# Releasing the loads of granules 8 and 9 by the last attention average instead of the landed transposes, in a fused attention and MoE kernel

## The chip, the cores and the metric

The kernel runs on one core of one Trainium2 chip. The metric is the device time of one execution in microseconds (us); lower is better. The kernel before takes 210.3 us (median of 3 runs, 210.06 to 210.32). A profiled execution has a span about 1.8 us shorter than its time, because the span begins with the first instruction of the program.

## The reference

Attention with a few global keys and a local window, then a two-layer MLP whose activation is `s * relu(x)^2 + b`. The attention is shortened here to its steps; the MLP is as in the reference:

```python
def _attn_ref(q, k, v, n_global, n_local):      # q, k, v: 4 x 8 x 768 x 64
    scores = (q @ k^T) / sqrt(64) + bias         # bias: -slope(head) * distance
    keep = first 8 keys, or the 96 keys up to the query's own
    a = softmax(where(keep, scores, -1e9))
    return a @ v

def _moe_ref(x, w_in, w_out, s, b):              # x: 3072 x 512, d_ff 2048
    h = x @ w_in
    r = np.maximum(h, 0.0)
    g = s * (r * r) + b
    return (g @ w_out).astype(np.float32)
```

## The kernel before

The 3072 tokens are cut into 12 granules of 256 (j = 0 to 11). Each granule passes through: loads of k, q and v from HBM (software DMA queue, issued by GpSimd, with a cast to bf16); transposes of k and q; scores, exponent and mask; weighted averages `xn[j]` (`stage_A`, normalised by VectorE, two heads at a time); transposes of `xn[j]` to `xT[j]`; the two MLP products. From granule 4 on the transposes are DMA transposes. They are issued by the sync engine (SP) on the hardware DMA queue, which also carries the stores of the output and the copies of v blocks (`vo`).

Six loads make a granule. They are issued four granules ahead, and from granule 6 on a *gate* holds them: a one-element copy on GpSimd that reads a tile, so that the loads behind it in GpSimd's order wait until that tile is written.

```python
    def load_granule(j):
        b, g = divmod(j, NGR)
        t = nat_tile(j)
        for i in range(GB):                        # GB = 2
            sb = g * GB + i
            for n in range(2):
                nc.gpsimd.dma_start(t[:, n, i, :, :], rows_of(srcs[n], b, sb))
            nc.gpsimd.dma_start(vbuf[b % 2][:, sb, :, 0:D], rows_of(v, b, sb))

    def hold_loads(ap):
        g = work.tile([P, 1], BF16, name="gate", tag="gate")
        nc.gpsimd.tensor_copy(g[0:1, :], ap)
...
    def x_by_dma(j):
        t = xT_tile(j)
        for i in range(GB):
            nc.sync.dma_start_transpose(t[:, :, i * P : (i + 1) * P], xn[j][:, i, :])
...
    def finish_granule(j):
        if j < X_PE:                               # X_PE = 4
            x_by_pe(j)
        else:
            x_by_dma(j)
        if 6 <= j + LEAD < NJ:                     # LEAD = 4, NJ = 12
            hold_loads(xT[j][0:1, 0, GT - 1 : GT])
            load_granule(j + LEAD)

    def step(s, c0, c1, c2, pool=None, pre=()):
        j = 2 * s // HP                            # two steps a granule
        last = (2 * s + 2) % HP == 0
        if not last and j >= 4 and j + 2 < NJ:
            qk_by_dma(j + 2)                       # 4 DMA transposes on SP
        ...
        if last:
            finish_granule(j)
            if SHIFT < j + 2 < NJ:
                load_voff(j + 2)
        ...
```

So the first MLP product of a granule waits for its pair `xT(j)`, and the gate of granule j+4 waits for the same pair.

The softmax here doesn't subtract the row's maximum and nothing guards it: scores larger than these inputs give would overflow.

## Time and profile before

| | before |
|---|---|
| time, median | 210.3 us |
| span of the profiled execution | 208.7 us |
| TensorE (PE) busy | 201.1 us, 96% |
| VectorE, ScalarE, GpSimd busy | 77%, 62%, 33% |
| PE idle for a pair xT | 1.13 us, once |

First the page of the kernel before: busy time, and the span in 40 slices of 5.2 us. A digit is the busy share in tenths. In all views PE is TensorE, PEld its weight loads, DVE VectorE, ACT ScalarE, POOL GpSimd and SPq the queue of SP; L616 is line 616 of the kernel, and x16 means 16 instructions in a row.

```profile
PE 201.1 (96%) x2183; PEld 160.0 (77%) x2191; DVE 160.0 (77%) x336; ACT 128.6 (62%) x200; POOL 68.9 (33%) x89
...
PE   6899999999999999999997999999999999999993
...
DMA  5999999999999999999999999999451210240006
...
DMA packets 110308, 28.17 MB, mean 135 GB/s; under 512 B 97836, under 2 KB 108780, under 8 KB 110284
```

TensorE bounds the kernel. The only dent of the PE row in the middle is the 7 of slice 22, at about 110 to 115 us. The DMA engines are busy over 90% of the time until about 145 us, although they move only 135 GB/s on average. The Trainium skill ("DMA: Bandwidth & Descriptors", Specifications) gives 512 B as the least transfer for line rate; 97,836 of the 110,308 packets here are smaller, which fits busy engines at a low rate.

The timeline of PE in that dent (start, duration, operation; in brackets the idle time before it and what ended it), then the chain that ended last in the same place (start, duration):

```profile
109.41 3.78 PE L816 MATMUL ps<-wsub,gsum 128*128 128x256 bf16 x32
...
114.57 1.91 PE L616 MATMUL ps<-xT,w_in_bf 128*128 128x256 bf16 x16 [1.13 <-DMA xT<-xn]
```

```profile
102.54 1.93 SPq L596
104.47 0.06 issue
104.53 9.90 DMA xT<-xn
114.44 0.14 issue
114.57 1.91 PE ps L616 x16
```

The second transpose of xT(6) was issued at 104.53 and took 9.90 us to land. PE was ready at 113.4 and started at 114.57. Next GpSimd (gates and first loads behind them) and SP:

```profile
81.63 0.18 POOL L122 COPY gate<-xT 1x1 bf16<-1x1 bf16 x1 [12.18 <-DMA xT<-xn]
82.20 0.87 POOL L116 DMA_DIRECT2D nat<-in_k_dram  x1 [0.40 <-issue]
...
96.01 0.26 POOL L122 COPY gate<-xT 1x1 bf16<-1x1 bf16 x1 [8.55 <-DMA xT<-xn]
96.61 0.88 POOL L116 DMA_DIRECT2D nat<-in_k_dram  x1 [0.34 <-issue]
...
114.56 0.18 POOL L122 COPY gate<-xT 1x1 bf16<-1x1 bf16 x1 [12.69 <-DMA xT<-xn]
```

```profile
76.30 2.51 SPq L596 DMA_TRANSPOSE xT<-xn  x2
...
90.05 2.54 SPq L596 DMA_TRANSPOSE xT<-xn  x2
```

The gate of granule 8 runs 5.3 us after the first transpose of xT(4) is issued, that of granule 9 6.0 us after that of xT(5). Last, the two DMA queues from 98 to 111 us (packets, MB, time of the packets as a share of this stretch on 16 engines; packets overlap, so over 100% is possible). q0 carries the loads, q1 transposes and stores:

```profile
q0 software_dynamic: 6213, 0.78, 111.4%
q1 hardware_dynamic: 2918, 1.14, 65.7%
```

In this stretch the loads of granule 9 took more of the engines than everything on the hardware queue.

### The profile page before, as it was taken

To read this page: it belongs to the slowest core of one execution; us is meant where nothing else is said; L and a number is where in the kernel's file an instruction comes from. 1 tells how busy PE (TensorE), PEld (TensorE's weight loads), DVE (VectorE), ACT (ScalarE), POOL (GpSimd) and SP (SyncE) were. 2 spreads that over 40 slices of the span, in tenths; PEclk is the share of its full clock that TensorE was granted. 3 is DMA by queue.
4 is the path that set the end of the run, shared out by engine and by line. 5 is a ranking of instruction groups with operands and counts; after the bars stand their busy time and mean duration, and the time that the engine had idled before them with its cause. 6 is when DMAs were issued, how large, how long until landed. Compare 5 with 4: busy or idle time off the path is not lost.

```text
span 208.7 us, 5315 instructions
## 1 busy us (share of the span) xinstructions
PE 201.1 (96%) x2183; PEld 160.0 (77%) x2191; DVE 160.0 (77%) x336; ACT 128.6 (62%) x200; POOL 68.9 (33%) x89
## 2 busy tenths in 40 slices
PE   6899999999999999999997999999999999999993
PEld 2677884557867585878886898888898889888883
DVE  7685689995989866799799784599785696737974
ACT  4975669485975558685763766564966665476200
POOL 8984334999646102705500906300000000000000
PEclk9999999999999999999999999999999999999999
DMA  5999999999999999999999999999451210240006
GB/s 167 170 181 206 207 207 172 155 152 135 115 147 143 155 157 193 120 265 188 145 207 128 113 133 174 184 208 100 52 158 49 77 28 0 50 154 0 0 4 200
DMA packets 110308, 28.17 MB, mean 135 GB/s; under 512 B 97836, under 2 KB 108780, under 8 KB 110284
## 3 DMA queue, kind: packets, MB, share of 16 engines
q0 software_dynamic: 75472, 13.11, 86.7%
q1 hardware_dynamic: 33612, 14.13, 39.0%
q10 hardware_dynamic: 1200, 0.59, 1.1%
q8 instruction: 17, 0.28, 0.6%
q14 instruction: 7, 0.06, 0.1%
HBM read 27.26 MB, written 6.29 MB: 161 GB/s over the span
## 4 chain that ended last, share of the span: by engine, by line
PE 76%; DMA 9%; POOL 4%; SPq 4%; DVE 3%; issue 1%; POOLq 0%
PE ps L616 35%; PE ps L816 19%; PE ps L664 13%; DMA xT<-xn 5%; DMA w_in_bf<-in_moe_w_in_dram 5%; PE ps_s L438 4%; PE ps_av L492 4%; SPq L357 3%; POOL nat L102 2%; POOL vb L108 2%; SPq L596 1%; PE ps_t L348 1%; POOL w_in_bf L140 1%; DVE o_early L697 1%; DVE wsub L751 1%
## 5 line engine op out<-in xcount | busy, mean ns | idle before, releaser
L616 PE MATMUL ps<-xT,w_in_bf 128*128 128x256 bf16 x768 | 90.5, 273 | 1.7 <-DMA xT<-xn 1.1
L626 ACT ACTIVATE gT<-ps 128x512 bf16<-128x512 f32 x96 | 55.7, 598 | 48.4 <-PE ps L616 48.2
L616 PEld LDWEIGHTS <-w_in_bf 128*128 128x128 bf16 x768 | 72.8, 98 | 11.3 <-issue 1.2
L447 ACT ACTIVATE pt<-ps_s 128x1024 bf16<-128x1024 f32 (+1 forms) x44 | 39.3, 946 | 3.2 <-PE ps_s L438 3.2
L664 PE MATMUL ps<-w_out_bf,gT 128*128 128x512 bf16 x120 | 28.9, 379 | 0.5 <-issue 0.2
L816 PEld LDWEIGHTS <-gsum 128*128 128x128 bf16 x256 | 24.1, 98 | 3.7 <-DVE gsum L779 0.5
L454 DVE TENSOR_TENSOR pt<-pt,tmpl 128x1024 bf16<-128x1024 bf16 (+1 forms) x40 | 24.5, 644 | 1.7 <-ACT pt L447 1.6
L790 DVE TENSOR_TENSOR gT<-gT 128x1024 bf16<-128x1024 bf16 x20 | 13.7, 685 | 11.6 <-ACT gT L626 11.6
L664 PEld LDWEIGHTS <-gT 128*128 128x128 bf16 x128 | 11.7, 98 | 13.2 <-issue 0.3
L463 DVE TENSOR_TENSOR xn<-ps_av,rc 128x256 bf16<-128x256 f32 x48 | 20.4, 424 | 1.7
L116 POOL DMA_DIRECT2D nat<-in_k_dram x20 | 17.7, 886 | 8.6 <-DMA w_in_bf<-in_moe_w_in_dram 2.1
L816 PEld LDWEIGHTS <-gT 128*128 128x128 bf16 x200 | 18.7, 98 | 2.3
L117 POOL DMA_DIRECT2D vb<-in_v_dram x20 | 18.4, 919 | 5.9 <-DMA nat<-in_k_dram 2.4
L116 POOL DMA_DIRECT2D nat<-in_q_dram x20 | 17.9, 896 | 6.9 <-DMA w_out_bf<-in_moe_w_out_dram 2.9
L462 DVE RECIPROCAL rc<-ps_av 128x4 f32<-128x4 f32 x48 | 8.6, 178 | 12.8 <-PE ps_av L492 10.6
L492 PEld LDWEIGHTS <-pt 128*128 128x128 bf16 x320 | 14.4, 98 | 2.7 <-DVE xn L463 0.7
L629 DVE TENSOR_TENSOR gT<-gT 128x512 bf16<-128x512 bf16 x32 | 13.0, 420 | 3.7 <-ACT gT L626 3.3
L492 PE MATMUL ps_av<-vb,pt 128*128 128x65 bf16 x208 | 15.4, 193 | 0.0
L816 PE MATMUL ps<-w_out_bf,gsum 128*128 128x256 bf16 x128 | 15.3, 273 | 0.0
L816 PE MATMUL ps<-wsub,gsum 128*128 128x256 bf16 x128 | 15.1, 273 | 0.0
L122 POOL COPY gate<-xT 1x1 bf16<-1x1 bf16 x6 | 1.1, 190 | 40.6 <-DMA xT<-xn 39.5
L816 PE MATMUL ps<-w_out_bf,gT 128*128 128x256 bf16 x120 | 13.9, 273 | 0.0
(112 smaller groups left out, 221.8 us busy)
## 6 DMA issues: line engine op xcount, KB each, us to landing
out_dram<-o_q SPq DMA_DIRECT2D x15, 256.0 KB, 2.3
vb<-in_v_dram POOLq DMA_DIRECT2D x24, 128.0 KB, 7.4
nat<-in_k_dram POOLq DMA_DIRECT2D x22, 128.0 KB, 6.9
nat<-in_q_dram POOLq DMA_DIRECT2D x22, 128.0 KB, 7.3
w_out_bf<-in_moe_w_out_dram POOLq DMA_DIRECT2D x4, 512.0 KB, 17.2
w_in_bf<-in_moe_w_in_dram POOLq DMA_DIRECT2D x3, 512.0 KB, 11.2
out_dram<-o_sb SPq DMA_DIRECT2D x4, 256.0 KB, 6.1
out_dram<-o_early SPq DMA_DIRECT2D x4, 256.0 KB, 5.2
```

What stands on the lines that cost most here:

```text
L116: nc.gpsimd.dma_start(t[:, n, i, :, :], rows_of(srcs[n], b, sb))
L117: nc.gpsimd.dma_start(vbuf[b % 2][:, sb, :, 0:D], rows_of(v, b, sb))
L447: nc.scalar.activation(pt[:, :, 0:ncol], ps[:, :, 0:ncol], ACT.Exp, scale=QSCALE)
L454: nc.vector.tensor_tensor(pv, pv, m.rearrange("p h a c -> p h (a c)"), ALU.mult)
L463: nc.vector.tensor_tensor(dst, av[:, :, :, 0:D], rc[:].to_broadcast((P, 2, 2, D)), ALU.mult)
L492: nc.tensor.matmul(av[:, i, hi, 0 : D + 1], lhsT=pt[:, hi, c * P : (c + 1) * P], rhs=vv, start=(n == 0), stop=(n == len(terms) - 1),)
L616: nc.tensor.matmul(ps[:, i, :], lhsT=w_in_bf[:, kc, fc * P : (fc + 1) * P], rhs=xT[j][:, kc, :], start=(kc == 0), stop=(kc == KC - 1),)
L626: nc.scalar.activation(gs, ps[:], ACT.Relu)
L629: nc.vector.tensor_tensor(gs, gs, gs, ALU.mult)
L664: nc.tensor.matmul(po[:], lhsT=g_of(j)[:, fc, tb * P : (tb + 1) * P], rhs=w_out_bf[:, fc, :], start=(fc == 0), stop=(fc == FC - 1),)
L790: outs.append(lambda: nc.vector.tensor_tensor(gs, gs, gs, ALU.mult))
L816: nc.tensor.matmul(ps[:, tb, cs], lhsT=stat[:, fc, tb * P : (tb + 1) * P], rhs=mov[:, fc, cs], start=(fc == 0), stop=(fc == NH - 1),)
```

## The change

The gates of granules 8 and 9 read the last normalised average of granules 4 and 5 instead of the landed transposes of it. The intent: these loads start some 5 us earlier, and are out of the way sooner. The instruction order of every engine stays the same.

```diff
         if 6 <= j + LEAD < NJ:
-            hold_loads(xT[j][0:1, 0, GT - 1 : GT])
+            if j in (4, 5):
+                hold_loads(xn[j][0:1, GB - 1, DM - 1 : DM])
+            else:
+                hold_loads(xT[j][0:1, 0, GT - 1 : GT])
             load_granule(j + LEAD)
```

## The prediction

> **What bounds the kernel.** The page gives TensorE (PE) 201.1 us busy of a 208.7 us span (96%), at full granted clock; VectorE 160.0 (77%), ScalarE 128.6 (62%). The chain of waits is nearly all PE. Only 7.6 us of PE idleness exists, mostly at head and tail. In the stage of the change (76 to 120 us), the timeline of PE shows one long gap: 1.13 us ahead of 114.57 us, where the first MoE product of granule 6 waits for the DMA transposes of xT(6). The list of waits has the same item (1.1 us, once), and the chain shows those transposes issued to 104.5 and landed at 114.44: 9.9 us. The same pair takes 2.4 to 2.5 us late in the kernel, when no loads run. So the reachable gain is about 1.1 us, 0.5%.
>
> **What moves.** The instruction order on every engine is unchanged; only what two 1-element gate copies on GpSimd wait for changes. No arithmetic is added or removed.
> - Gate of granule 8: now at 81.63 us (landed xT(4)); it should run at about 76.3, when the last average of granule 4 is done. Its six loads (0.87 to 0.93 us issue each, now 82.2 to 87.4) move to about 76.9 to 82.2: 5.3 us earlier.
> - Gate of granule 9: now 96.01; should run near 90.1. Loads move from 96.6-101.9 to about 90.7-96: 5.9 us earlier.
> - Later gates still wait for landed transposes, but these land earlier if xT(6) does.
>
> **Gain.** Loads of granule 9 occupy the software DMA queue from 98 to about 110 us now, on top of xT(6) (issued 102.5 to 106). Moved by 6 us, they should be nearly done by 104; xT(6) then lands at about 108 to 110, before PE wants it (113.4). The 1.13 us wait goes. Gate 10 runs then, near 109 instead of 114.6, and xT(7) (6.9 us to landing now, slack over 4 us) gets easier too; no gain there, PE does not wait for it.
>
> **Cost.** The two pairs of transposes that used to be protected now share the DMA engines with the loads. The Trainium skill ("DMA: Bandwidth & Descriptors", "Queues, rings and completion order") says each DMA engine round-robins between its queues packet by packet; the trace agrees in effect: pairs beside running loads land in 4.5 to 9.9 us, pairs without in 2.4.
> - xT(4): second transpose issued at 77.55, landed at 81.6 (4.0 us; the tail of granule 7's loads ends near 79.2). PE wants it at 84.04. With loads continuing, I estimate 6 to 7 us (like xT(7) 6.9 and xT(8) 6.2): 83.5 to 84.6, so a new wait of 0 to 1 us, 0.4 expected.
> - xT(5): issued to 92.6, landed 95.9, wanted at 98.5. Loads ran beside it before too (granule 8's tail to 93.7). Estimate 97 to 98: no or a small wait.
> - The score transposes of granules 7 and 8 land later, with slack of many us. Buffers of the loads (query/key slots of granules 4 and 5, value blocks) are read out well before 76 and 90 us, so no new wait.
>
> **Sum.** -1.1 + 0.4 + 0.1 = -0.6 us: 210.3 to 209.7 us. Range 208.9 to 210.9. Faster by over 2%: 1%; within 2%: 97%; slower: 2%.
>
> **What would show it.** Gate copies at about 76.3 and 90.1; first software-queue packets of granule 8 near 78; the wait of PE for xT at 114 gone; xT(6) landing within 7 us; a PE gap of under 1 us near 84 with xT(4) as releaser.
>
> **What would make it wrong.** xT(4) or xT(5) landing in about 10 us as xT(6) does now: 2 to 4 us lost. Or another wait right behind xT(6)'s, such as a PSUM buffer, taking the gain. Or later pairs (xT(7), xT(8)) falling onto granule 10's and 11's loads at a worse moment.

## More of the kernel before

From 103 to 115 us:

```profile
q1 hardware_dynamic: 3682, 1.54, 95.7%
q0 software_dynamic: 3437, 0.43, 65.9%
```

From 104.53 to 114.43 us, while the second transpose of xT(6) was under way, the shares were 101.7% (q1) and 49.5% (q0), and from 110 to 115 us only 38 load packets ran. So the wait for xT(6) is not only a matter of loads beside it: the last score transposes and the stores ahead of it landed only at 105.2 to 111.0 us, and a copy of v blocks (`vo`), issued right behind it at 106.12 us, landed with it at 114.4.

## The result, and the profile after

The changed kernel took 209.9 us (median of 4 runs, 209.44 to 210.0) beside 210.31 us (210.06 to 210.74): ratio 0.9974, 95% interval 0.9952 to 0.9996. A ratio here is the mean time of one kernel's fast runs over that of the other's of the same rounds, so it is not quite the ratio of the medians.

The span fell from 208.7 to 208.1 us. The same lines as before, first the page:

```profile
PE 202.3 (97%) x2183; PEld 160.5 (77%) x2191; DVE 160.5 (77%) x336; ACT 128.8 (62%) x200; POOL 69.5 (33%) x89
...
PE   7999999999999999999999999999999999999993
```

The dent is gone. The timeline of PE at xT(5) and xT(6), without a bracket now:

```profile
99.11 1.92 PE L616 MATMUL ps<-xT,w_in_bf 128*128 128x256 bf16 x16
...
114.00 1.91 PE L616 MATMUL ps<-xT,w_in_bf 128*128 128x256 bf16 x16
```

The gates, the loads, and the pairs on SP:

```profile
76.80 0.31 POOL L122 COPY gate<-xn 1x1 bf16<-1x1 bf16 x1 [6.67 <-DVE xn L463]
77.40 0.88 POOL L116 DMA_DIRECT2D nat<-in_k_dram  x1 [0.29 <-issue]
...
89.47 0.57 POOL L122 COPY gate<-xn 1x1 bf16<-1x1 bf16 x1 [6.81 <-DVE xn L463]
90.09 0.88 POOL L116 DMA_DIRECT2D nat<-in_k_dram  x1
...
112.01 0.52 POOL L122 COPY gate<-xT 1x1 bf16<-1x1 bf16 x1 [16.66 <-DMA xT<-xn]
```

```profile
100.27 3.21 SPq L357 DMA_TRANSPOSE qx<-nat  x1
...
104.75 2.55 SPq L596 DMA_TRANSPOSE xT<-xn  x2
```

The two gates run 4.8 and 6.5 us earlier. And the queues from 98 to 111 us:

```profile
q1 hardware_dynamic: 4066, 1.87, 100.6%
q0 software_dynamic: 3452, 0.43, 55.0%
```

In this stretch the loads moved 0.43 MB instead of 0.78, and the hardware queue 1.87 MB instead of 1.14.

The trace has the time at which the semaphore of each DMA reached its full count. Worked out from it, for the second transpose of each pair: from issue to landing, and the slack, from landing to the start of the first product that reads the pair.

| pair | before: landing after, slack | after: landing after, slack |
|---|---|---|
| xT(4) | 4.0 us, 2.47 us | 6.0 us, 0.54 us |
| xT(5) | 4.5 us, 2.60 us | 7.0 us, 0.05 us |
| xT(6) | 9.9 us, 0.13 us (PE waited) | 5.8 us, 2.11 us |
| xT(7) | 6.9 us, 4.39 us | 7.1 us, 4.94 us |
| xT(8) | 6.7 us, 3.47 us | 4.1 us, 6.14 us |

For xT(8) before, the prediction has 6.2 us; the full count gives 6.7. A slack of 0.05 to 0.13 us is the time from landing to start when PE is released by the landing itself. So the changed kernel has moved the thin place from xT(6) to xT(5): it starts those products just as they arrive.

How to compare two spans: the two traces differ by 0.46 us before the change can act. The last group of sixteen first-layer products of granule 3, a point ahead of the first moved gate, starts at 75.43 us before and at 75.89 after. I use it as a mark. **From the mark to the end** it takes 133.28 us before and 132.24 after: 1.04 us less. The span shows only 0.6 of it, because the profiled execution of the changed kernel happened to reach the mark later. Over the 14 traces, with the same instructions up to the mark on every engine that computes (eight PE records are missing in some traces), the mark lies between 75.25 and 76.09 us.

### The profile page after: what moved, and what is told of

Same layout as the page of the kernel before. It is cut to its first block, busy times and chain, and to the rows that moved or that the text cites. A ratio compares the mean times of both kernels' runs of the same rounds, so it can differ in the third digit from the quotient of the medians.

```text
span 208.1 us, 5315 instructions
## 1 busy us (share of the span) xinstructions
PE 202.3 (97%) x2183; PEld 160.5 (77%) x2191; DVE 160.5 (77%) x336; ACT 128.8 (62%) x200; POOL 69.5 (33%) x89
## 4 chain that ended last, share of the span: by engine, by line
PE 86%; DMA 5%; POOL 4%; DVE 3%; issue 1%; POOLq 0%
PE ps L616 40%; PE ps L816 24%; PE ps L664 12%; DMA w_in_bf<-in_moe_w_in_dram 5%; PE ps_s L438 4%; PE ps_av L492 4%; POOL nat L102 2%; POOL vb L108 2%; POOL w_in_bf L140 1%; PE ps_t L348 1%; DVE wsum L642 1%; DVE pt L454 1%; PE ps_last L816 0%; PE ps_x L588 0%; DVE vo L394 0%
## 5 line engine op out<-in xcount | busy, mean ns | idle before, releaser
L616 PE MATMUL ps<-xT,w_in_bf 128*128 128x256 bf16 x768 | 90.4, 273 | 0.3 <-DMA w_in_bf<-in_moe_w_in_dram 0.3
L616 PEld LDWEIGHTS <-w_in_bf 128*128 128x128 bf16 x768 | 72.7, 98 | 10.0 <-DMA w_in_bf<-in_moe_w_in_dram 0.5
L116 POOL DMA_DIRECT2D nat<-in_k_dram x20 | 17.7, 886 | 8.3 <-DMA w_in_bf<-in_moe_w_in_dram 2.0
L117 POOL DMA_DIRECT2D vb<-in_v_dram x20 | 17.9, 894 | 5.5 <-DMA nat<-in_k_dram 2.0
L492 PEld LDWEIGHTS <-pt 128*128 128x128 bf16 x320 | 14.5, 97 | 3.0 <-DVE xn L463 0.7
L792 ACT ACTIVATE gT<-gT 128x1024 bf16<-128x1024 bf16 x12 | 12.7, 1057 | 0.4
```

The lines of the kernel that those rows point to most:

```text
L492: nc.tensor.matmul(av[:, i, hi, 0 : D + 1], lhsT=pt[:, hi, c * P : (c + 1) * P], rhs=vv, start=(n == 0), stop=(n == len(terms) - 1),)
L616: nc.tensor.matmul(ps[:, i, :], lhsT=w_in_bf[:, kc, fc * P : (fc + 1) * P], rhs=xT[j][:, kc, :], start=(kc == 0), stop=(kc == KC - 1),)
```

## The experiments

Theory T1: the gain is the end of PE's wait for xT(6), which came from granule 9's loads on the DMA engines while the hardware queue in front of xT(6) drained; the price is slack at xT(4) and xT(5). Rival R1: it helps that all loads come earlier. Rival R2: the difference is start-up scatter. After the first eight runs T1 was sharpened to T2: in the timed runs the changed kernel gives part of its gain back, since the thin slacks run out in some executions.

Every result below was correct. "To the end" is from the mark to the end; the ratio is to the kernel before on the same chip.

| run | to the end, us | PE gap at a pair xT | slack of xT(4), (5), (6), us | median us, range | ratio, 95% interval |
|---|---|---|---|---|---|
| before_again | 133.15 | xT(6) 0.99 | 3.40, 1.68, 0.13 | 210.01, 209.22 to 210.88 | 1.0001, 0.9972 to 1.0031 |
| after_again | 132.22 | none | 0.81, 0.05, 3.01 | 209.80, 209.40 to 211.24 | 1.0006, 0.9975 to 1.0037 |
| only9 | 132.54 | xT(5) 0.46 | 2.68, 0.05, 1.93 | 210.12, 209.76 to 210.31 | 1.0007, 0.9985 to 1.0028 |
| only8 | 132.07 | none | 0.74, 3.04, 0.13 | 210.01, 209.25 to 211.13 | 1.0009, 0.9978 to 1.0040 |
| extra_loads | 133.46 | xT(4) 0.74, xT(6) 0.36 | 0.13, 0.05, 0.13 | 211.00, 210.22 to 211.74 | 1.0030, 1.0001 to 1.0058 |
| late9 | 132.05 | none | 2.44, 2.67, 2.80 | 209.51, 209.23 to 209.73 | 0.9956, 0.9936 to 0.9975 |
| both_at_4 | 132.14 | none | 1.31, 0.05, 2.67 | 210.16, 209.88 to 210.35 and one of 214.38 | 0.9984, 0.9963 to 1.0006 |
| split9 | 132.32 | xT(4) 0.12, xT(5) 0.09 | 0.13, 0.05, 1.99 | 210.17, 209.35 to 210.47 | 0.9979, 0.9955 to 1.0003 |
| after_third | 132.22 | none | 0.81, 0.05, 3.42 | 210.25, 209.36 to 211.89 | 1.0000, 0.9962 to 1.0037 |
| late9_again | 132.64 | xT(8) 0.44 | 2.60, 2.49, 0.54 | 209.74, 209.23 to 210.24 | 0.9967, 0.9936 to 0.9998 |
| early8_late9 | 132.09 | none | 0.72, 3.61, 1.96 | 209.89, 209.14 to 211.32 | 0.9980, 0.9945 to 1.0015 |
| late9_extra | 132.05 | none | 2.99, 0.48, 1.31 | 209.96, 209.40 to 211.28 | 0.9984, 0.9950 to 1.0017 |

Each row has one trace and six timed runs; the trace is of the first of the six. Rows 1 to 4, 5 to 8 and 9 to 12 ran together on one chip each. The 214.38 us run is over 1.5% above the kernel's fastest, so slow, and is left out of the ratio.

### before_again and after_again: both kernels once more

No edit.

> Control: the kernel before, unchanged. All theories: ratio 1.000 within 0.2%. Its trace is a second look at the kernel before: theory T1 (the whole gain is the end of PE's wait for xT(6)) expects a PE gap ahead of the first product of granule 6 of 0.5 to 1.5 us again, xT(6) landing 8 us or more after its issue, and 133.3 +- 0.4 us from the last products of granule 3 (75.4 us) to the end. The rival R2 (the difference is start-up scatter) expects that this stretch varies by as much as the 1.04 us that separate the first two traces.

> The changed kernel again, for the size of the gain. T1: ratio 0.994 to 0.998, no PE gap for xT(6), 132.2 +- 0.3 us from the last products of granule 3 to the end, slack of xT(5) under 0.5 us. R2: ratio 0.999 to 1.001.

The traces repeat: the kernel before has the gap again, the changed kernel has not.

```profile
114.66 1.91 PE L616 MATMUL ps<-xT,w_in_bf 128*128 128x256 bf16 x16 [0.99 <-DMA xT<-xn]
```

To the end: 133.28 and 133.15 us before, 132.24, 132.22 and (after_third) 132.22 after. The two kernels are apart by seven times the difference between the repeats, so R2 fails for the profiled executions. The timed runs do not follow: the ratio was 1.0006 here and 1.0000 in after_third, after 0.9974 at first. T1's 0.994 to 0.998 is missed. The single times of the changed kernel reach 211.24 and 211.89 us, those of the kernel before, in the three chip sessions, 210.88, 211.33 and 211.57.

### only9 and only8: one half of the change at a time

```diff
-            if j in (4, 5):
+            if j in (5,):          # only9;  (4,) for only8
```

> Only granule 9's loads are released by the average (granule 5); granule 8's still by the landed xT(4). T1: this half alone carries the gain, since the loads beside xT(6) are those of granule 9: ratio as after_again within 0.15%, no PE gap at xT(6), xT(4) landing about 4 us and with its slack of about 2.5 us back. Rival R1 (both loads must come earlier, as a queue that is cleared from granule 8 on): half of the gain or less.

> Only granule 8's loads are released by the average (granule 4); granule 9's still by the landed xT(5). T1: nearly no gain, ratio 0.998 to 1.000, PE gap at xT(6) of 0.5 us or more stays, because granule 9's loads still start near 95 to 96 us. R1: half of the gain (gap about 0.5 us).

only9 removes the gap at xT(6) and gives xT(4) its slack back, as T1 said, but xT(5) then arrives 7.7 us after its issue and PE waits there:

```profile
99.45 1.92 PE L616 MATMUL ps<-xT,w_in_bf 128*128 128x256 bf16 x16 [0.46 <-DMA xT<-xn]
```

The loads of granule 8, landing until 94.8 us, and those of granule 9, issued from 89.9, now both lie beside xT(5). So "this half carries the whole gain" was too simple: about 0.7 of the 1.0 us remains (133.28 and 133.15 before, 132.54 here). only8 contradicts T1 outright: I expected a gap of 0.5 us or more, and there was none; xT(6) landed 9.0 us after its issue, but just in time. Its loads of granule 9 were all landed by 107.9 us, against 114.3 and 112.3 in the two traces of before, though issued at nearly the same time (96.2 against 96.6 and 97.8). Clearing granule 8 early also helps the next set through; R1 has a point there. One trace of each cannot say how often, and the trace of only8 is of the fastest of its six runs (209.25 us, median 210.01), as are those of both_at_4 and split9. The timed runs separate neither from the kernel before.

### extra_loads: two more loads beside xT in the changed kernel

```diff
+    spare = [const.tile([P, H, D], BF16, name=f"spare{i}", tag=f"spare{i}") for i in range(2)]
...
             load_granule(j + LEAD)
+            if j == 4:
+                for n in range(2):     # to spare tiles, not used
+                    nc.gpsimd.dma_start(spare[n][:], rows_of(srcs[n], 3, n))
```

> The changed kernel with two needless loads of 128 KB (to a spare tile) behind the six of granule 8, so that the software queue stays busy about 2.5 us longer, to about 91 to 94 us, just ahead of xT(5). T1 (the changed kernel has no slack left at xT(5): 0.05 us in two profiles): xT(5) lands 1 to 3 us late, PE shows a gap of 0.5 to 2.5 us near 99 to 101 us, 133.2 to 134.5 us from the last products of granule 3 to the end; ratio to before 1.000 to 1.007. Rival (the loads run in free time and PE does not feel them): no gap, 132.2 us, ratio as the changed kernel.

The cost came, 133.46 to the end, 1.24 us over the changed kernel, and the timed ratio is 1.003. The place was partly wrong: the gaps are at xT(4) and xT(6), not at xT(5), which again arrived just in time, after PE had been held up already. (This kernel has one line more, so L617 is L616 elsewhere.)

```profile
84.81 1.91 PE L617 MATMUL ps<-xT,w_in_bf 128*128 128x256 bf16 x16 [0.74 <-DMA xT<-xn]
...
114.83 1.91 PE L617 MATMUL ps<-xT,w_in_bf 128*128 128x256 bf16 x16 [0.36 <-DMA xT<-xn]
```

The two loads landed at 95.3 and 98.3 us, later than the 91 to 94 us expected. So PE does feel the loads, and the changed kernel has no room for more of them.

### late9: the loads of granule 9 later than before

```diff
+        if j == 6:
+            hold_loads(xn[6][0:1, GB - 1, DM - 1 : DM])
+            load_granule(9)
-        if 6 <= j + LEAD < NJ:
+        if 6 <= j + LEAD < NJ and j != 5:
             hold_loads(xT[j][0:1, 0, GT - 1 : GT])
             load_granule(j + LEAD)
```

> The opposite direction: granule 8's loads as before, granule 9's loads released later than before, by the last average of granule 6 (about 102 us in place of 96). T1 in its simple form (what hurts xT(6) is loads that run while the hardware queue in front of it, score transposes of granule 8 and two stores, drains): that queue drains alone, score transposes of granule 8 land by about 103, xT(6) beside the loads takes 6 to 7 us from about 104.3, lands at 110.5 to 111.5, no PE gap, 132.2 to 132.5 us to the end. Rival R1 (only an earlier release helps; later loads meet xT(6) more): xT(6) lands at 114 or later, gap of 1 us or more, 133.2 us or more to the end.

> The late release of granule 9 again. T2: every pair xT has 2 us or more to spare, so its runs are tight (spread under 0.8 us) and faster: ratio to before 0.994 to 0.997, median 0.2 to 0.8 us under that of after_third. If the first late9 result was the chance of one chip: ratio 0.998 to 1.001, no better than after_third.

This was the run that told most. The gate of granule 9 moves 5.7 us the other way, from 96.01 to 101.67, so that its loads begin together with xT(6) and run beside it to its landing, and the gap is gone all the same:

```profile
101.67 0.51 POOL L122 COPY gate<-xn 1x1 bf16<-1x1 bf16 x1 [13.91 <-DVE xn L463]
```

The score transposes of granule 8, ahead of xT(6) in the hardware queue, had landed by 102.5 us (107.2 before), and the two stores behind them by 104.5 (111.0 before); xT(6) then took 6.9 us, although the loads took 115.5% of the engines in that time, against 49.5% while it was under way before. The timeline of PE at xT(6), without a gap, and the queues from 98 to 111 us in late9, where the loads take 64.0% in place of 111.4%, much as in the changed kernel (55.0%):

```profile
113.56 1.91 PE L616 MATMUL ps<-xT,w_in_bf 128*128 128x256 bf16 x16
```

```profile
q0 software_dynamic: 3735, 0.47, 64.0%
q1 hardware_dynamic: 3210, 1.25, 59.5%
```

R1, which wanted 133.2 us or more, fails as the sole reason: loads need not come early. That they must not meet a backlog on the other queue fits this trace, but it is not the whole account. The other three traces with late loads also had the queue ahead clear by 105.4 us, and there xT(6) took 7.7, 8.1 and 8.9 us (early8_late9, late9_extra, late9_again), the last not far from the 9.3 and 9.9 us of before. And the changed kernel gets there by another way than T1 says: its score transposes and stores landed at 108.0 and 110.7 us, no sooner than before, but while its xT(6) was under way the loads took only 4.2% of the engines.

In late9 the three pairs keep 2.4 us or more, its six runs lie within 0.5 us, and it is the fastest kernel: 0.9956, and 0.9967 on another chip, both intervals below 1. It is no free lunch: in late9_again xT(6) had only 0.54 us left, the runs were spread over 1.01 us where T2 expected less than 0.8, and later traffic was pushed onto xT(8), which took 10.6 us.

```profile
144.72 1.91 PE L616 MATMUL ps<-xT,w_in_bf 128*128 128x256 bf16 x16 [0.44 <-DMA xT<-xn]
```

### both_at_4 and split9: earlier still, and in two parts

both_at_4 puts the loads of granule 9 right behind those of granule 8; split9 releases three loads of granule 9 by the average of granule 5 and three by the landed xT(5).

```diff
# both_at_4
-        if 6 <= j + LEAD < NJ:
-            hold_loads(xT[j][0:1, 0, GT - 1 : GT])
+        if 6 <= j + LEAD < NJ and j != 5:
+            if j == 4:
+                hold_loads(xn[4][0:1, GB - 1, DM - 1 : DM])
+            else:
+                hold_loads(xT[j][0:1, 0, GT - 1 : GT])
             load_granule(j + LEAD)
+            if j == 4:
+                load_granule(9)
# split9, in place of load_granule(9)
+                load_qk(9, 0)
+                load_v(9, [0])
+                hold_loads(xT[5][0:1, 0, GT - 1 : GT])
+                load_qk(9, 1)
+                load_v(9, [1])
```

> The loads of granules 8 and 9 both released by the average of granule 4 (about 76.7), twelve loads in a row to about 87 us, landing until about 98. T1: xT(4) as in the changed kernel (slack 0.4 to 1.0), xT(5) beside loads until about 97, lands at 98 to 100, PE gap 0 to 1 us there; xT(6) free of loads, 3 to 5 us to landing, slack 4 us or more; 132.2 to 133.2 us to the end, so between the two kernels. R1 (earlier is better throughout): 132.2 or less, no gap.

> Granule 8 by the average of granule 4 as in the changed kernel; of granule 9 the first three loads by the average of granule 5, the other three by the landed xT(5). A try at the best of both halves: T1: xT(5) lands at 96 to 98 (slack 1 to 2.5), xT(6) at 111 to 112.5 (slack 1 to 2), no PE gap, 132.2 us to the end, and fewer slow executions than the changed kernel if its 210.7 to 211.2 us runs come from xT(5); ratio 0.996 to 0.999.

In both_at_4 the loads lasted until 106.8 us, not 98, and still xT(6) had 2.7 us of slack, xT(5) none: 132.14 to the end, no better than the changed kernel. split9 did not do what I wanted: xT(5) got no slack, with granule 8's loads landing until 94.3 us and three of granule 9's beside it, and xT(4) had a gap of 0.12 us. Neither is a better kernel than late9.

### after_third, early8_late9 and late9_extra: where the changed kernel loses in the timed runs

early8_late9 is late9 with granule 8 released as in the changed kernel. late9_extra is late9 with the two needless loads of extra_loads. The edits are those above, combined.

> The changed kernel a third time, beside late9_again on the same chip. T2 (in the timed runs the changed kernel gives part of its gain back because xT(4) and xT(5) arrive with 0.0 to 0.8 us to spare, so an execution in which they are a little later stalls): ratio to before 0.996 to 1.000, spread of its runs 0.7 us or more, profile: 132.0 to 132.6 us from the last products of granule 3 to the end.

> The changed release of granule 8 (average of granule 4) with the late release of granule 9. This separates the two thin slacks of the changed kernel: xT(4) is beside loads as in the changed kernel (slack 0.1 to 0.8), xT(5) is free (slack 3 or more), xT(6) as in late9. T2: profile 132.0 to 132.4 us to the end; runs a little slower or more scattered than late9_again (ratio 0.995 to 0.999) if xT(4) causes the slow executions, equal to late9_again if they come from xT(5) alone.

> The late release with the same two needless loads behind those of granule 8 that cost the changed kernel 1.2 us in its profile. T2 (a load costs time only where it eats more than the slack of the transposes beside it): xT(4) untouched (slack 2 or more), xT(5) loses 1 to 3 of its 2.7 us, xT(6) as in late9; PE gap 0 to 0.3 us, 132.0 to 132.5 us to the end, ratio to late9_again within 0.15%. Rival (every added load costs PE time through the shared DMA engines): 133 us or more to the end, 0.4% or more over late9_again, as it did in the changed kernel.

late9_extra is the clean comparison, though with one trace: the loads that cost the changed kernel 1.24 us to the end cost late9 nothing (132.05, as late9). They took xT(5) down to 0.48 us of slack and stopped there. That is what T2 says, and the rival (every load costs) fails in this trace; in the timed runs the ratios of late9_extra and late9_again, 0.9984 and 0.9967, differ by 0.17%, just over the 0.15% expected and well inside their intervals. early8_late9 shows where each slack went: with granule 8 early alone, xT(4) is down to 0.72 us as in the changed kernel, but xT(5) has 3.61. On the slow executions T2 stays unproved: early8_late9 and late9_extra each had one run of six over 211.2 us, the changed kernel 2 of 16 (4 of 16 over 210.6), late9 none of 12. But the kernel before, counted in the same way over all sessions, had 2 of 43 over 211.2 us and 9 of 43 over 210.6, so long runs are not special to the changed kernel. These counts are too small to name xT(4) or xT(5), and none of the runs over 211.2 us was profiled.

## Why the prediction was right or wrong

The prediction said 209.7 us, 208.9 to 210.9, and within 2%; 209.9 was measured. Point by point:

- **What bounds it, and the reachable gain: right.** PE at 96%, one gap of 1.13 us at xT(6). In the traces the change takes 1.04 us from the stretch after the mark.
- **The gates: right.** Predicted at about 76.3 and 90.1, found at 76.80 and 89.47. The first loads were issued at 77.40 and 90.09.
- **xT(4): size right, consequence too dark.** Predicted to land in 6 to 7 us and to cost 0.4 us; it took 6.0 us and arrived 0.54 us before it was wanted, with no gap in three traces of the changed kernel.
- **xT(5): mis-sized.** Predicted to land at 97 to 98; it landed at 99.06 (98.6 if the late start is taken off), with all of its slack gone. The failed step is the term "loads ran beside it before too", from which I took the loads of granule 9 for no worse than the tail of granule 8's. They are worse, since they run on through the whole of its flight. In the seven traces in which granule 9's loads start beside xT(5) or earlier (the changed kernel three times, only9, split9, extra_loads, both_at_4) its second transpose takes 6.9 to 7.7 us; in the six where they start after its landing (before twice, only8, late9 twice, early8_late9) 3.4 to 5.5. early8_late9 shows that in the changed kernel it is these loads and not the earlier granule 8: with granule 8 as in the changed kernel and granule 9 late, xT(5) takes 3.4 us. Whose loads they are does not matter: in the fourteenth trace, late9_extra, granule 9 starts late too, but the two needless loads land until 98.2 us, and xT(5) takes 6.6 us. The waiting itself is small: against the mark, its products start 0.17 us later than in the kernel before (99.11 - 75.89 against 98.48 - 75.43), and 0.02 and 0.08 us in the two repeats, so the "0.1" of the sum was about right.
- **xT(6): mechanism right, size off.** The loads no longer lay on top of it (4.2% of the engines while it was under way, 49.5% before), and the wait went; late9 shows that this is not the only way to end it. It was to land at 108 to 110; it landed at 111.9. The loads of granule 9 lasted until 107.7 us, not 104: first issue to last landing took 17.6 us, as it had before (17.7 us). And SP issued the second transpose at 106.04, 1.5 us later than before, since one score transpose of granule 8 held it for 3.21 us (1.29 before; 3.42 and 3.08 in the repeats of the changed kernel, 1.23 in that of the kernel before). The gate of granule 10 ran at 112.0 instead of 109.
- **Sum: near the predicted -0.6 us in the first comparison, in part by luck.** There the means differ by about 0.55 us (0.26%) and the medians by 0.4. In the profiled executions the change is worth -1.04 us, not -0.6, because the expected 0.4 us at xT(4) did not come; the profiled execution reached the mark 0.46 us late, which has nothing to do with the change. In timed runs the three comparisons gave 0.9974, 1.0006 and 1.0000, whose mean of 0.9993 is about -0.1 us, less than predicted. So the 0.26% of the first comparison is not established, and that it came near the prediction is luck as far as these runs show. Where 1 us of gain goes in the unprofiled executions is open. That thin slack eats it fits the traces (0.05 us at xT(5) in all three) and the late9 kernel, but it is an argument, not shown. A rival is that the traces make the kernel before look worse than it is: both its profiled executions (210.51 and 210.57 us) are above the medians of their sessions (210.3 and 210.0), those of the changed kernel (209.9, 209.8 and 210.0) at or below theirs (209.9, 209.8 and 210.25). Against it, late9 removes the same gap and gains about 0.7 and 0.9 us in timed runs (0.9967 and 0.9956), so the wait seems to be there in them too.

The Trainium skill ("DMA: Bandwidth & Descriptors", Queues, rings and completion order) has each DMA engine serve its queues in turn, packet by packet. The traces agree in effect: in the kernel before, the second transpose of a pair takes 2.5 us with no loads about (xT(10), xT(11); 3.7 for xT(9), with copies of v blocks beside it) and 4.0 to 9.9 us beside loads (xT(4) to xT(8)). The same page says under "Issuing engines are not separate DMA queues" that DMAs of different engines share the same 16 DMA engines and interleave; that is why a load issued by GpSimd can hold up a transpose issued by SP at all. late9_extra agrees: two more loads from GpSimd, and xT(5), issued by SP, took 6.6 us in place of 4.5 and 4.6 in the late9 traces.

## What to carry to other kernels

When a gate for prefetches is moved, list the slack of every transfer that lies beside the new place, not only of the one that the move is to relieve: here a wait of 1 us was removed, and about 2 and 2.5 us of slack at two other places were spent for it. Look also at the transfers ahead of it in its own queue: here a transpose arrived late when loads had run beside these, and shifting the loads either way, even later, freed it. The later release was the better one here, faster than the kernel before in both timed comparisons, and it kept the slack at xT(4) and xT(5), though at xT(6) not always. For effects under 1 us measure from a common point ahead of the change in the traces, and repeat the timed comparison before believing a quarter of a per cent.

## What the Trainium skill lacked or had wrong

- "DMA: Bandwidth & Descriptors" (Queues, rings and completion order) tells how queues share an engine, but has no figure for a DMA transpose beside software-queue loads. In these runs the second transpose of a pair landed after 2.5 to 4.2 us without loads, and after 3.1 to 10.6 us with them.
- The same page's fit for one DMA on the software path (Anatomy of one DMA), 2.0 us plus bytes over 436e3, would give 2.3 us for a load of 128 KB (an estimate from that page). Here the median of the k, q and v loads was 6.9 to 7.4 us, in the trace of the kernel before, and the set of six of granule 9 took 17.7 us from first issue to last landing there, 14.5 in the repeat. The loads cast, come in packets under 512 B and share the engines; the page gives no figure for such a case.
